# First unit of a gated linear-attention kernel: products of raw neighbours, summed on TensorE and scaled afterwards

## The chip, the cores and the metric

The kernel runs on one core of a Trainium2 chip. That core has five engines, each with its own list of instructions: PE (TensorE, the matrix unit, with PEld for its weight loads), DVE (VectorE), ACT (ScalarE), POOL (GpSimd) and SP (SyncE, which here only issues DMAs). They run side by side and wait for one another by semaphores. The metric is the device time of one execution, in microseconds (us).

## The reference

Two parts follow each other. The first is a recurrence over 768 steps for 4 batches and 8 heads of width 48, with a complex gate per step and channel; the second multiplies its output (3072 rows of 384) by two matrices with a squared ReLU between.

```python
mag = np.sqrt(a_re * a_re + a_im * a_im)
scale = np.minimum(mag, 0.999) / (mag + 1e-06)
a_re_n, a_im_n = (a_re * scale, a_im * scale)
for t in range(S):
    ar, ai = (a_re_n[:, :, t, :, None], a_im_n[:, :, t, :, None])
    new_re = ar * S_re - ai * S_im
    new_im = ar * S_im + ai * S_re
    kv = np.einsum('bhd,bhe->bhde', k[:, :, t], v[:, :, t])
    S_re, S_im = (new_re + kv, new_im)
    y[:, :, t] = np.einsum('bhd,bhde->bhe', q[:, :, t], S_re)
# x: y as 3072 rows of 384
h = x @ w_in
r = np.maximum(h, 0.0)
return (r * r) @ w_out
```

## The kernel before

**Units.** The 3072 rows are cut into six units of 512, `n` = 0 to 5. A unit lies on 128 partitions with four neighbouring steps on each (`c` = 0 to 3) and is treated in two halves of four heads, `z` = 0 and 1. Since a step is a product with a complex gate, a chunk of steps needs the running products of the gates. The kernel forms them in stages:

- `roots(z)`: from the gate `a` (tile `aq`: re and im, 768 elements each per half) the inverse root of its squared length, by squares (L998 on DVE, L993 on ACT), a sum (L1001), logarithm, exponential and square on ACT (L1003, L1005, L1008), and one refining step on DVE (L1011, L1015).
- `normalise(z)`: the scale, from three copies with a factor on ACT (L1021, L1028, L1030) and a minimum times a factor on DVE (L1032); then `a` times the scale (L1035, 1536 wide).
- `inner(z)`: each pair of neighbouring steps multiplied: four real products by L1050 (as two instructions) and their sum and difference by L1054 and L1055; then the product of the two pairs, of which unit 0 forms only the terms on DVE.
- `totals`: in unit 0 PE adds those terms and turns them (`joint`, L1125, with the permuted identity `perm` and its negative); ACT copies the outcome into `e` (L1136, L1139).
- `scan`: 128 totals are multiplied up along the partitions in short steps on DVE (L1211 to L1282). PE turns the outcome back (`back`, L1104, copied by L1303), giving `xn`.
- `moved`: a row of `e` needs the value of the partition before it. Four DMAs on SP's queue (L1195) copy `xn`, shifted by one partition, into `e`; the first partition is set by POOL (L1189). `factors` forms an inverse (L1152 to L1167) whose row moves the same way.
- `inverse` (L1069, L1074), `twist` (L1081) and `apply` (L1351 to L1379) use `e` on `a`, q and k; the last of them write the products to `f`.

Then `pairs` turns those products (in unit 0 on PE, L1494, copied by ACT L1497), multiplies them to scores (L1516), masks them on DVE (L1522), and mixes them with v and the states (L1574, L1578) into `xT`. `dense` follows with w_in (L1634, on `xT`), the squared ReLU on ACT (L1666, L1667), and w_out (L1681 in unit 0, L1743 in the others; these replace one product in eight by sums on DVE, L1758 and L1767).

**Weights.** They arrive as 64-bit floats in 16 pieces, which are fetched on POOL's queue (L826) into buffers that are free then, and converted: the low word on ACT (L839), the sign and top of the mantissa on ACT (L843) or, for the last two pieces, on DVE (L849), the rest on DVE (L845, L852).

**What sets the order.** Every step is recorded by `step` with an assumed duration, the keys it reads and writes, and a rank; `Plan.order` lays all of them out as a list per engine, taking on each engine the step of lowest rank among those it thinks ready. The table at the end of `fast_path` (`plan.shift`) moves single steps and groups of steps by changing their ranks. Where PE would stop for a while, `Plan.emit` writes idle products of `ident` by `ident` (L744) into PE's list; they are real instructions and cannot be skipped. On the chip each engine works off its list in that order.

## Time and profile before

| | us |
|---|---|
| median of three runs (lowest, highest) | 669.27 (668.72, 670.49) |
| profiled execution, its own time | 669.19 |
| span of that execution on the core | 667.5 |
| PE busy, of the span | 648.7 |
| DVE busy | 555.4 |
| ACT busy | 380.1 |
| POOL busy | 155.9 |

The profile counts time from the start of the span. An engine is busy while an instruction of its runs; a matmul of 32-bit floats leaves two records, so counts of PE are twice the instructions of the lists shown below. A row of the timeline gives the start, the duration, the engine, the source line, the operation with output<-inputs, shape and count, and, in brackets, how long the engine had stood idle and what ended that. In the table of stretches the columns are, for each stretch, its length, then busy time and instructions of each engine, TensorE's granted clock (1.00 is full speed), the DMA engines' busy share and GB/s.

### The profile page before, as it was taken

The numbers are of one execution on the slowest core, as the hardware profiler recorded it, in microseconds if no ns is written. First come the engines' busy times: TensorE is split into PE (matmuls) and PEld (weight loads), VectorE is DVE, ScalarE is ACT, GpSimd is POOL, SyncE is SP. The second block draws the span as 40 slices with busy tenths as digits, with TensorE's granted clock in tenths as the row PEclk, the third lists the DMA queues.
The fourth block names the chain that finished last, engine by engine and source line by source line (L and its number), as shares of the span: only waits on it lengthen the run. The fifth ranks groups of instructions, "written<-read, shape, count | busy, mean of one in ns | idle before, by whom it ended". The sixth has DMA issues, their size and how long they took to land.

```text
span 667.5 us, 13612 instructions
## 1 busy us (share of the span) xinstructions
PE 648.7 (97%) x5176; PEld 586.9 (88%) x5176; DVE 555.4 (83%) x1137; ACT 380.1 (57%) x640; POOL 155.9 (23%) x253
## 2 busy tenths in 40 slices
PE   9989999999999899999999999999999999999995
PEld 9988888676768898998989999989989989989995
DVE  6999999999599999888998989997889995248631
ACT  6998589935766336658356558157577253141320
POOL 6321565042110022031143051130040210042100
PEclk9999999999999999999999999999999999999998
DMA  6953649157730136433157253174260243188500
GB/s 201 352 162 103 142 118 319 27 119 168 189 96 1 35 90 157 111 100 91 36 136 177 69 130 69 42 181 126 61 167 25 73 111 83 57 315 275 190 7 25
DMA packets 34948, 82.40 MB, mean 123 GB/s; under 512 B 7956, under 2 KB 13600, under 8 KB 34872
## 3 DMA queue, kind: packets, MB, share of 16 engines
q0 software_dynamic: 17024, 58.60, 31.0%
q1 hardware_dynamic: 15672, 20.63, 12.2%
q10 hardware_dynamic: 2176, 2.20, 1.2%
q8 instruction: 43, 0.70, 0.5%
q14 instruction: 33, 0.27, 0.1%
HBM read 48.76 MB, written 4.72 MB: 80 GB/s over the span
## 4 chain that ended last, share of the span: by engine, by line
PE 66%; DVE 21%; DMA 5%; issue 2%; SPq 1%; ACT 1%; POOL 1%; DVEq 0%; POOLq 0%; ACTq 0%
PE d L1634 28%; PE d L1743 27%; PE sc L1516 3%; PE yp L1574 3%; DVE f L1379 2%; PE yp L1578 2%; DVE f L1050 2%; DMA QT<-aq 2%; PE tr L1546 2%; DMA e<-xn 2%; DVE w L852 1%; DMA aq<-in_q_dram 1%; DVE aq L1035 1%; DVE KC L1231 1%; DVE aq L1463 1%
## 5 line engine op out<-in xcount | busy, mean ns | idle before, releaser
L1634 PE MATMUL d<-xT,w 128*128 128x256 f32 x1104 | 245.9, 380 | 0.4 <-ACT ot L1686 0.4
L1634 PEld LDWEIGHTS d<-xT,w 128*128 128x128 f32 x1104 | 208.0, 190 | 30.5 <-ACT ot L1686 0.8
L1666 ACT ACTIVATE g<-d 128x512 f32<-128x512 f32 x92 | 55.0, 598 | 138.5 <-PE d L1634 122.4
L1743 PE MATMUL d<-w,g 128*128 128x192 f32 x640 | 110.6, 326 | 0.0
L1743 PEld LDWEIGHTS d<-w,g 128*128 128x128 f32 x640 | 104.9, 190 | 0.5
L1743 PE MATMUL d<-T,g 128*128 128x192 f32 x480 | 85.8, 329 | 0.0
L1743 PEld LDWEIGHTS d<-T,g 128*128 128x128 f32 x480 | 78.5, 190 | 1.3 <-DVE ot L1767 0.4
L1758 DVE TENSOR_TENSOR g<-g 128x512 f32<-128x512 f32 x80 | 54.0, 689 | 25.0 <-PE d L1743 19.5
L1704 POOL DMA_DIRECT2D out_dram<-ot x22 | 12.5, 567 | 214.5 <-DVE ot L1767 184.1
L1667 ACT ACTIVATE g<-g 128x512 f32<-128x512 f32 x96 | 60.6, 631 | 3.1
L744 PE MATMUL d<-ident 128*128 128x128 f32 x484 | 56.9, 280 | 1.7 <-POOL ident masks.py:199 1.7
L744 PEld LDWEIGHTS d<-ident 128*128 128x128 f32 x484 | 56.1, 196 | 1.9 <-POOL ident masks.py:199 1.7
L1463 DVE STREAM_TRANSPOSE aq<-f 128x768 f32<-128x768 f32 x40 | 47.9, 1278 | 0.2
L1584 ACT COPY yt<-yp 112x512 f32<-112x512 f32 x24 | 26.6, 1110 | 36.3 <-PE yp L1578 36.1
L1423 POOL DMA_DIRECT2D KC<-f x56 | 35.1, 634 | 47.5 <-DVE f L1379 24.4
L1681 PE MATMUL d<-w,g 128*128 128x384 f32 x128 | 44.0, 491 | 1.7 <-ACT g L1667 1.5
L1379 DVE TENSOR_TENSOR f<-aq 128x768 f32<-128x768 f32 (+1 forms) x56 | 43.9, 838 | 0.5
L1466 ACT COPY QT<-aq 32x512 f32<-32x512 f32 x57 | 35.2, 618 | 8.9 <-DVE aq L1463 6.6
L1522 DVE TENSOR_TENSOR A<-sc,mask 128x512 f32<-128x512 f32 x45 | 29.9, 691 | 12.4 <-PE sc L1516 12.1
L1767 DVE TENSOR_TENSOR ot<-ot,d 128x192 f32<-128x192 f32 x70 | 23.6, 349 | 17.9 <-PE d L1743 17.2
L1681 PEld LDWEIGHTS d<-w,g 128*128 128x128 f32 x128 | 23.7, 190 | 16.5 <-ACT g L1667 1.9
L1516 PE MATMUL sc<-QT 96*64 96x128 f32 (+1 forms) x736 | 37.0, 251 | 0.0
(201 smaller groups left out, 995.6 us busy)
## 6 DMA issues: line engine op xcount, KB each, us to landing
QT<-aq SPq DMA_DIRECT2D x152, 64.0 KB
f<-in_moe_w_in_dram POOLq DMA_DIRECT2D x8, 768.0 KB, 6.7
f<-in_moe_w_out_dram POOLq DMA_DIRECT2D x8, 768.0 KB, 6.7
out_dram<-ot POOLq DMA_DIRECT2D x22, 192.0 KB, 2.2
KC<-f POOLq DMA_DIRECT2D x20, 192.0 KB, 3.9
xT<-yt SPq DMA_DIRECT2D x36, 96.0 KB
aq<-in_q_dram POOLq DMA_DIRECT2D x8, 384.0 KB, 4.5
aq<-in_k_dram POOLq DMA_DIRECT2D x8, 384.0 KB, 5.4
```

The source lines that it names most:

```text
L744: plan = Plan(lambda b: pe.matmul(bank[b][:, 0:C], lhsT=ident, rhs=ident, start=True, stop=True), ["d2", "d1", "d0"], lambda ap: tc.nc.val ...
L1379: lambda j=j, r=r, o=o: dve.tensor_tensor(out=o[:, :, :, r * D:(r + 1) * D], in0=qk[:, j], in1=a[:, r], op=ALU.mult), late[z])
L1423: lambda i=i, queue=queue, lo=lo, hi=hi, a0=a0, a1=a1: queue.dma_start(out=kc[lo:hi, i], in_=nat[a0:a1]),
L1463: lambda nat=nat, dst=dst, j=j: dve.transpose(out=dst[:, j], in_=nat), rank)
L1466: lambda b=b, t=t, T6=T6: act.copy(out=t[32 * b:32 * b + 32, b], in_=T6[32 * b:32 * b + 32, i % 2, b]),
L1516: pe.matmul(sa[r:r + C // 2, j, :, lo:32], lhsT=T[:, j, 1, h, ts(late, C // 2)], rhs=T[:, j, 0, h].rearrange("p (c t) -> p c t", c=W)[:, : ...
L1634: pe.matmul(ps, lhsT=w1[:, f // FP, m, ts(f % FP, C)], rhs=xT[:, n % 2, m, ts(grp, G)], start=(m == 0), stop=(m == NM - 1))
L1666: act.activation(out=o, in_=ps, func=AF.Relu)
L1667: act.activation(out=o, in_=o, func=AF.Square)
L1681: pe.matmul(ps, lhsT=gt[:, f % 2, ts(i, C)], rhs=w2[:, f], start=(f == 0), stop=(f == NF - 1))
L1743: pe.matmul(bank[b][:, 0:DH], lhsT=g4[:, r, j], rhs=w(j), start=first and j == 0, stop=last and j == NT - 1)
L1758: step("DVE", tt(4 * C), gk(x0, h) + gk(x1, h), gk(o, h), lambda: dve.tensor_tensor(out=g4[:, o, sl], in0=g4[:, x0, sl], in1=g4[:, x1, sl] ...
```

## The change

All of it but three edits concerns unit 0.

1. `raw_products`: the neighbours' four real products are formed from the gates as loaded, among the steps of `roots`. PE adds them in PSUM with `ident` and its negative (two matmuls of 384 columns for each of re and im, per half). Once the scale is known, `scaled_products` multiplies the scales of the two neighbours and then the sums from PSUM by that. L1035 is gone in unit 0; the first neighbour of each pair is scaled in `first_factors`, which comes with the steps behind the scan.
2. `normalise`, all units: one copy with a factor and an offset and one minimum times it give the scale, so one of three copies on ACT (L1030) is gone.
3. `roots`, unit 0: the second half's square of the real part goes from DVE to ACT.
4. `moved`, unit 0: `e`'s three rows come from PE, by a matmul with an identity that is shifted by one column (`after`, 384 columns each), and a copy by ACT that adds the first partition's constant (`top`). Four DMAs and three POOL memsets are gone, while POOL sets up `after` and `top` at the start.
5. `convert`: the last two pieces of w_out are converted like the others, with L843 on ACT in place of L849 on DVE.
6. A new table of shifts, so a new order in all units, with the fetches in another order too.

```diff
@@ set-up
+    after = yts[1][:, C:2 * C]
+    top = yts[1][:, 2 * C:2 * C + 3]
+    pool.memset(after[:, 0:1], 0.0)
+    pool.tensor_copy(out=after[:, 1:C], in_=ident[:, 0:C - 1])
+    for j, x_ in enumerate((SCALE, 0.0, SCALE ** -2)):
+        pool.memset(top[:, j:j + 1], 0.0)
+        pool.memset(top[0:1, j:j + 1], x_)
@@ convert
-        mixed = i < 2 * NPIECE - 2
-        if mixed:
-
-            step("ACT", 1.68, keys + [("lo", i)], [("lo", i, 1)], lambda: act.activation(
-                out=part(F16, 1), in_=part(I16, 3), func=AF.Copy, scale=2.0 ** -60), rank)
+        step("ACT", 1.68, keys + [("lo", i)], [("lo", i, 1)], lambda: act.activation(
+            out=part(F16, 1), in_=part(I16, 3), func=AF.Copy, scale=2.0 ** -60), rank)
...
-        if not mixed:
-            step("DVE", tt(PW), keys + wk, wk, lambda: dve.scalar_tensor_tensor(
-                out=bits, in0=hi, scalar=0xC0000000, in1=bits,
-                op0=ALU.bitwise_and, op1=ALU.bitwise_or), rank)
@@ new functions
+        def raw_products(z):
+
+            t = (KC[0][:, 0:2 * Y] if z == 0 else xT[:, 0].rearrange("p m t -> p (m t)"))
+            keys = K if z == 0 else [("xT", 0, m) for m in range(NM)]
+            f = t.rearrange("p (j r g d) -> p j r g d", j=2, r=2, d=D)
+            cut = 2 if z == 0 else 1
+            for u in range(cut):
+                gs = ts(u, W * HH // 2 // cut)
+                x0, x1 = (halves(z)[:, :, gs, y] for y in range(2))
+                for j in range(2):
+                    step("DVE", tt(Y // cut), [("a", z, "r", r, u) for r in range(2)], keys,
+                         lambda x0=x0, x1=x1, j=j, gs=gs: dve.tensor_tensor(
+                             out=f[:, j, :, gs], in0=x0, in1=x1[:, j].unsqueeze(
+                                 1).to_broadcast(list(x0.shape)), op=ALU.mult), first)
+            fx = t.rearrange("p (j r x) -> p j r x", j=2, r=2)
+            for r in range(2):
+                b = ("sc0", "sc1", "tr0", "tr1")[2 * z + r]
+
+                def go(r=r, b=b):
+                    pe.matmul(bank[b][:, 0:DM], lhsT=ident, rhs=fx[:, 0, r], start=True,
+                              stop=False)
+                    pe.matmul(bank[b][:, 0:DM], lhsT=ident if r else minus, rhs=fx[:, 1, 1 - r],
+                              start=False, stop=True)
+                step("PE", 1.3, keys + ([] if r else [("yt", 1)]), [(b,)], go, first)
+
+        def scaled_products(z):
+            sc = col[z][1].rearrange("p (g y d) -> p g y d", y=2, d=D)
+            step("DVE", tt(Y // 2), key(z, 1), key(z, 1), lambda: dve.tensor_tensor(
+                out=sc[:, :, 1], in0=sc[:, :, 0], in1=sc[:, :, 1], op=ALU.mult), first)
+            for r in range(2):
+                b = ("sc0", "sc1", "tr0", "tr1")[2 * z + r]
+                step("DVE", tt(Y // 2) + 0.06, [(b,)] + key(z, 1), [("a", z)],
+                     lambda r=r, b=b: dve.tensor_tensor(
+                         out=halves(z)[:, r, :, 1],
+                         in0=bank[b][:, 0:DM].rearrange("p (g d) -> p g d", d=D),
+                         in1=sc[:, :, 1], op=ALU.mult), first)
+
+        def first_factors(z):
+            sc = col[z][1].rearrange("p (g y d) -> p g y d", y=2, d=D)
+            for r in range(2):
+                step("DVE", tt(Y // 2), [("a", z)] + key(z, 1), [("a", z)], lambda r=r: dve.tensor_tensor(
+                    out=halves(z)[:, r, :, 0], in0=halves(z)[:, r, :, 0], in1=sc[:, :, 0],
+                    op=ALU.mult), late[z])
@@ normalise
             step("ACT", ac(Y), key(z, 3), key(z, 0), lambda: act.activation(
-                out=f0, in_=t, func=AF.Copy, scale=0.999), first)
+                out=f0, in_=t, func=AF.Copy, scale=-0.999e-6, bias=0.999), first)
+            scale = f1 if n == 0 else f0
+            step("DVE", tt(Y), key(z, 0, 3), key(z, 1 if n == 0 else 0),
+                 lambda: dve.scalar_tensor_tensor(
+                     out=scale, in0=t, scalar=1.0 / 0.999, in1=f0,
+                     op0=ALU.min, op1=ALU.mult), first)
...
-            step("ACT", ac(Y), key(z, 2), key(z, 1), lambda: act.activation(
-                out=f1, in_=f2, func=AF.Copy, scale=-1.0, bias=2.0), first)
-            step("DVE", tt(Y), key(z, 0, 1), key(z, 0), lambda: dve.scalar_tensor_tensor(
-                out=f0, in0=f0, scalar=1.0, in1=f1, op0=ALU.min, op1=ALU.mult), first)
+            if n == 0:
+                scaled_products(z)
+                return
@@ moved
+            if n == 0:
+                for j in range(rs.start, rs.stop):
...
+                    step("PE", 0.65, ([("xn", 2, i) for i in range(6)] if j == 2 else
+                                      [("xn", j, z) for z in range(2)]) + [("yt", 1)], [(b,)],
+                         lambda j=j, ps=ps: pe.matmul(ps, lhsT=after, rhs=xn[:, j], start=True,
+                                                      stop=True), rk)
+                    step("ACT", ac(DM), [(b,), ("yt", 1)], [("e", j)],
+                         lambda j=j, ps=ps: act.activation(
+                             out=e.rearrange("p r w g -> p r (w g)")[:, j], in_=ps,
+                             func=AF.Identity, bias=top[:, j:j + 1]), rk)
+                return
@@ table of shifts
-        groups={4: 0.43, 15: 436.02, 16: 7.67, 22: 100.25, 29: -247.66, 33: 0.01, 49: 210.38, 69:
+        groups={11: -98.48, 13: 462.32, 15: 462.32, 16: 443.82, 18: -237.52, 81: -141.6, 84: 547.15,
...
```

The change adds lines, so what was L744 is L751 in the lists of the new kernel, L1035 is L1085, L1050 is L1100, L1125 is L1183, L1211 is L1283, L1351 is L1422, L1104 is L1162; L1032, L1040, L1042, L1048, L1053, L1061 and L1251 there are the new products, sums, scalings and the matmul for `e`.

**PE, from the start to `joint`.** In these rows `d` is the bank of the idle products, `f` and `perm` belong to the first matmuls of `joint`, and `tr_112`, `tr_113` are the banks of the totals. Before, from the first instruction:

```order
L744 MATMUL d_109<-ident 128x128 x121
L1125 MATMUL tr_112<-perm,f_70 64x16x8 x2
L1125 MATMUL tr_112<-yt_89,f_70 64x16x8 x2
L1125 MATMUL tr_112<-perm,f_70 64x16x8
L1125 MATMUL tr_112<-perm,f_71 64x16x8
L1125 MATMUL tr_112<-yt_89,f_70 64x16x8
```

With the change, from the first instruction (the banks `sc` and `tr` hold the sums of the raw products of the first and the second half; `KC` and `xT` hold the products):

```order
L751 MATMUL d_109<-ident 128x128 x34
L1040 MATMUL sc_110<-KC_75,ident 128x384
L1042 MATMUL sc_110<-KC_75,yt_90 128x384
L1040 MATMUL sc_111<-KC_75,ident 128x384
L1042 MATMUL sc_111<-KC_75,ident 128x384
L751 MATMUL d_109<-ident 128x128 x3
L1040 MATMUL tr_112<-xT,ident 128x384
L1042 MATMUL tr_112<-xT,yt_90 128x384
L1040 MATMUL tr_113<-xT,ident 128x384
L1042 MATMUL tr_113<-xT,ident 128x384
L751 MATMUL d_109<-ident 128x128 x28
L1183 MATMUL tr_112<-perm,f_70 64x16x8 x2
```

One run of 121 idle products stood ahead of `joint`. Now 34, 3 and 28 stand there, with eight matmuls of 384 columns between.

**PE, from the totals to the first turn of unit 0's products (L1494 before, L1567 now).** Before:

```order
L744 MATMUL d_109<-ident 128x128 x47
L1104 MATMUL tr_112<-ident,xn 128x128 x3
L744 MATMUL d_109<-ident 128x128 x3
L1104 MATMUL tr_113<-ident,xn 128x128 x3
L744 MATMUL d_109<-ident 128x128 x64
L1494 MATMUL d_107<-ident,f_70 96x128 x4
```

With the change:

```order
L751 MATMUL d_109<-ident 128x128 x46
L1162 MATMUL tr_112<-ident,xn 128x128 x3
L751 MATMUL d_109<-ident 128x128 x3
L1162 MATMUL tr_113<-ident,xn 128x128 x3
L1251 MATMUL tr_112<-xn,yt_90 128x384
L751 MATMUL d_109<-ident 128x128 x4
L1251 MATMUL tr_113<-xn,yt_90 128x384
L751 MATMUL d_109<-ident 128x128 x25
L1251 MATMUL tr_112<-xn,yt_90 128x384
L751 MATMUL d_109<-ident 128x128 x32
L1567 MATMUL d_107<-ident,f_70 96x128 x4
```

`e`'s three rows are matmuls now (L1251), and 110 idle products stand where 114 stood.

**DVE, between the roots and the product of the two pairs, unit 0.** `f` holds roots and scales, `aq` the gates. Before:

```order
L1069 SCALAR_TENSOR_TENSOR f_70<-f_70 128x4x144
L1032 SCALAR_TENSOR_TENSOR f_70<-f_70 128x768
L1035 TENSOR_TENSOR aq_68<-aq_68,f_70 128x1536
L1050 TENSOR_TENSOR f_70<-aq_68 128x768 x2
L1032 SCALAR_TENSOR_TENSOR f_71<-f_71 128x768
L1069 SCALAR_TENSOR_TENSOR f_71<-f_71 128x4x144
L1035 TENSOR_TENSOR aq_69<-aq_69,f_71 128x1536
L845 TENSOR_SCALAR w_66<-KC_76 128x768
L1050 TENSOR_TENSOR f_71<-aq_69 128x768 x2
L1054 TENSOR_TENSOR aq_68<-f_70 128x8x48
L1055 TENSOR_TENSOR aq_68<-f_70 128x8x48
```

With the change:

```order
L1032 TENSOR_TENSOR KC_75<-aq_68 128x2x192 x2
L1000 TENSOR_TENSOR f_71<-f_71 128x768
L1010 SCALAR_TENSOR_TENSOR f_70<-f_70 128x384
L1014 SCALAR_TENSOR_TENSOR f_70<-f_70 128x384
L1032 TENSOR_TENSOR xT<-aq_69 128x768 x2
L1010 SCALAR_TENSOR_TENSOR f_71<-f_71 128x768
L1014 SCALAR_TENSOR_TENSOR f_71<-f_71 128x768
L1071 SCALAR_TENSOR_TENSOR f_70<-f_70 128x768
L1048 TENSOR_TENSOR f_70<-f_70 128x8x48
L849 TENSOR_SCALAR w_66<-g 128x768
L1053 TENSOR_TENSOR aq_68<-sc_110,f_70 128x8x48
L1053 TENSOR_TENSOR aq_68<-sc_111,f_70 128x8x48
```

The raw products of the second half (`xT`) now stand ahead of the last steps of its root, those of the first half earlier still; where L1035 and the neighbours' products and sums stood, there are the scale (L1071), the product of two scales (L1048) and two products with PSUM (L1053). One conversion (L849, L845 before) stands in both.

More of the change, by code (lines that the diff above doesn't have):

```diff
@@ L768, in dma @@
     def dma(q, reads, writes, fn, rank, size, lat=1.8, group=None, dur=None):
-        name, took = ("POOL", 0.67) if q is pool else ("SP", 0.62) if q is sp else ("ACT", 0.53)
+        name, took = ("POOL", 0.67) if q is pool else ("SP", 0.62) if q is sp else ("ACT", 0.6)
         step(name, dur or took, reads, writes, fn, rank, (lat, size), group)
@@ L1083, in chain @@
         E = [("e", 0), ("e", 1), ("e", 2)]
-        nperm = yts[0][:, 0:C]
-        for fn in (roots, normalise, inner):
+        K = [(k_, 0, q_) for k_ in ("KC", "KC0", "KC1") for q_ in range(2)]
+        nperm, minus = (yts[i][:, 0:C] for i in range(2))
+        if n == 0:
+            for i, by in ((1, ident), (0, perm)):
+                step("ACT", 0.25, [], [("yt", i)], lambda i=i, by=by: act.mul(
+                    out=yts[i][:, 0:C], in_=by, mul=-1.0), rank)
+            for z in range(2):
+                roots(z)
+                raw_products(z)
+        for fn in (roots, normalise, inner)[n == 0:]:
             for z in range(2):
                 fn(z)
-                if n == 0 and z == 0 and fn is normalise:
-                    step("ACT", 0.25, key(0, 1), [("yt", 0)], lambda: act.mul(
-                        out=nperm, in_=perm, mul=-1.0), rank)
         ps_ = parts(n)
```

46 lines of the change are left out of this document (27 added, 19 removed), and 37 rows, old and new, of tables (groups, single).

## The prediction

> **What bounds the kernel now.** I read the busy totals first, then the table of stretches, since an average over the run hides stages with different limits.
>
> ```profile
> PE 648.7 (97%) x5176; PEld 586.9 (88%) x5176; DVE 555.4 (83%) x1137; ACT 380.1 (57%) x640; POOL 155.9 (23%) x253
> core 0: us, PE busy (x) PEld busy (x) DVE busy (x) ACT busy (x) POOL busy (x), PEclk, DMA share, GB/s
> 0.00:16.00 16.00, 14.35 (x114) 14.35 (x115) 9.47 (x15) 10.81 (x20) 10.84 (x30) 1.00 0.64 196
> 16.00:55.30 39.30, 37.60 (x357) 36.95 (x357) 37.50 (x86) 37.82 (x54) 11.09 (x19) 1.00 0.78 253
> 55.30:90.10 34.80, 32.59 (x498) 29.70 (x496) 34.26 (x93) 23.30 (x34) 15.85 (x22) 1.00 0.47 108
> 110.00:230.00 120.00, 114.65 (x750) 88.83 (x749) 108.94 (x235) 79.84 (x141) 20.58 (x34) 1.00 0.41 106
> 230.00:660.00 430.00, 429.66 (x3372) 399.72 (x3370) 345.67 (x686) 209.93 (x365) 84.89 (x131) 1.00 0.41 113
> ```
>
> PE's 97% is misleading until its work is named. The timeline of PE shows that for the first 62 us it mostly multiplies ident by ident (L744), which nobody reads:
>
> ```profile
> 1.65 28.84 PE L744 MATMUL d<-ident 128*128 128x128 f32 x242 [1.65 <-POOL ident masks.py:199]
> 30.42 0.44 PE L1125 MATMUL tr<-perm,f 128*64 128x128 f32 x4
> 47.22 14.46 PE L744 MATMUL d<-ident 128*128 128x128 f32 x128
> 62.68 1.96 PE L1494 MATMUL d<-ident,f 128*96 128x128 f32 x16 [1.00 <-DVE f L1379]
> 90.13 1.99 PE L1634 MATMUL d<-xT,w 128*128 128x256 f32 x8
> ```
>
> The dense work starts at 90.13. From 230 to 660 PE idles 0.34 us of 430, and 5.35 us of 120 between 110 and 230. So the span is the time to 90.13, then PE's list, then a tail; what brings the start of the list forward shortens the run, as long as PE is fed. Before 90 the limit is DVE: 37.50 busy of 39.30, then 34.26 of 34.80. Its milestones, from the timeline of DVE:
>
> ```profile
> 4.22 0.56 DVE L998 TENSOR_TENSOR f<-aq 128x384 f32<-128x384 f32 x1 [2.73 <-DMA aq<-in_a_im_dram]
> 5.55 0.56 DVE L998 TENSOR_TENSOR f<-aq 128x384 f32<-128x384 f32 x1 [0.77 <-DMA aq<-in_a_im_dram]
> 8.39 1.83 DVE L998 TENSOR_TENSOR f<-aq 128x768 f32<-128x768 f32 x2 [1.14 <-DMA aq<-in_a_im_dram]
> 13.96 0.96 DVE L1011 SCALAR_TENSOR_TENSOR f<-f 128x768 f32<-128x768 f32 x1 [0.63 <-ACT f L1008]
> 35.46 0.35 DVE L1211 TENSOR_TENSOR KC<-e 128x192 f32<-128x192 f32 x1
> 46.12 0.66 DVE L1282 TENSOR_TENSOR xn<-KC 128x288 f32<-128x288 f32 x1
> 55.32 1.43 DVE L1351 TENSOR_TENSOR f<-aq,e 128x192 f32<-128x192 f32 x5 [0.49 <-DMA e<-xn]
> 87.12 1.27 DVE L1522 TENSOR_TENSOR A<-sc,mask 128x512 f32<-128x512 f32 x2
> ```
>
> The scan runs from 35.46 to 46.78, the use of e starts at 55.32, the last mask of unit 0 ends at 88.39, and PE needs 1.74 us more to the dense work.
>
> **The change, part by part.** Durations, from the groups with each shape apart (columns: count, busy us and mean ns of one):
>
> ```profile
> L1035 DVE TENSOR_TENSOR aq<-aq,f 128x1536 f32<-128x1536 f32 x12 | 21.1, 1756 | 0.4
> L1054 DVE TENSOR_TENSOR aq<-f 128x384 f32<-128x384 f32 x12 | 6.7, 555 | 0.3
> L998 DVE TENSOR_TENSOR f<-aq 128x768 f32<-128x768 f32 x2 | 1.8, 954 | 1.1 <-DMA aq<-in_a_im_dram 1.1
> L852 DVE CUSTOM_DVE_ANT_0 w<-T,w 128x1536 uint16<-128x1536 uint16 x5 | 4.7, 957 | 0.0
> L845 DVE TENSOR_SCALAR w<-w 128x768 uint32<-128x768 uint32 x5 | 2.7, 551 | 0.0
> L849 DVE SCALAR_TENSOR_TENSOR w<-T,w 128x768 uint32<-128x768 uint32 x2 | 1.9, 966 | 0.1
> L1081 DVE TENSOR_TENSOR aq<-aq,f 128x576 f32<-128x576 f32 x12 | 8.7, 750 | 0.0
> ```
>
> Neighbours on DVE overlap by about 0.085 us (the two of 768 at 8.39 take 1.83, not 1.91), so one counts as 1.67, 0.47, 0.87, 0.87, 0.47, 0.88 and 0.67 us in the order of these rows.
>
> *Ahead of the scan, removed:* two L1035 (3.34), four neighbour sums L1054/L1055 (1.88), one square that goes to ACT (0.87): 6.09. *Added:* two products of scales and four scaled neighbours, all 384 wide (6 x 0.47 = 2.82), and 0.14 because the first half's two raw products are cut in four: 2.96. The raw products themselves are the old L1050, moved ahead. Net -3.1. *Idle time:* the four waits above are 5.27 us. The first (2.73) is for data and stays. With raw products in the list, of the others about 0.2 (ACT's square) and 0.8 (the second half's data at 8.39, DVE through its list at about 7.6) are left, and L1011 no longer waits: -1.5. *Put off:* in the new order one L845 and two L852 fewer stand ahead of the scan (-2.2), and one L1081 more (+0.7). Together -6.1: scan at 29.4.
>
> PE has its own floor there, as its idle products are a fixed list. Their price is 28.84/242 per record, two records each, 0.238 us. The wide matmul's price comes from a row of the dense stage:
>
> ```profile
> 113.56 4.04 PE L1681 MATMUL d<-w,g 128*128 128x384 f32 x12
> ```
>
> Two records each again: 0.66 us for 128x384. The eight sums of raw products cost 5.3 us, the 65 idle products left ahead of the perm matmuls 15.5; with the start at 1.65 and some 2.2 us of waiting for the raw products the floor is 24.6, where DVE's last operand (L1100) is also due. From 30.42 to the scan the old kernel took 5.04; so 29.6, and I take that: **-5.9**. Unseen is how late the raw products come: a microsecond late passes on as one, since the 28 idle products behind them can't be skipped. Bounds -0.3 and +2, taken 0.
>
> The four scaled neighbours read PSUM on DVE; the nearest rows are 128x512 with PSUM and without:
>
> ```profile
> L1522 DVE TENSOR_TENSOR A<-sc,mask 128x512 f32<-128x512 f32 x45 | 29.9, 691 | 12.4 <-PE sc L1516 12.1
> L1758 DVE TENSOR_TENSOR g<-g 128x512 f32<-128x512 f32 x80 | 54.0, 689 | 25.0 <-PE d L1743 19.5
> ```
>
> 691 against 689: no surcharge is taken. [...]
>
> *Scan to the use of e.* Added: four L1061 (1.88, half of the scaling that L1035 did). One L1081 is gone (-0.7), and the 0.49 wait. Conversions: as many as before. Net +0.7: first use at 50.1, **-5.2**. The four DMAs are only worth that 0.49, not the 7.1 us from their issue to 55.32:
>
> ```profile
> 48.20 8.07 SPq L1195 DMA_DIRECT2D e<-xn  x4
> ```
>
> DVE filled that time with conversions and the factors, which remain. e through PE and ACT (0.66 and a copy of 0.5 per row of e) must be there by 50.1: in ACT's list the first two copies stand behind the logarithm, the exponential and one sum of squares, about 3 us after DVE's first factor steps end near 45.7, so at 48.9; the third stands behind one conversion, at 52, and the k products want it at about 53. Bounds: 0, or +1.5 if ACT is late by half a conversion's pair; taken 0.
>
> *To the last mask.* One L852 more stands ahead of it: +0.87, so **-4.3**, and dense at 85.8. ACT now has four conversions (an L839 and an L843, some 2.65 each) between e and the copies of the turned products; from 48.9 it is through at about 60. PE's idle products and DVE's first f hold the first turn until about 58.5, it takes 1.96 (the row at 62.68), so ACT comes when it is just over: 0, at worst +0.5.
>
> *Behind 90.* The last two pieces of w_out lose L849 (-1.9 on DVE) and cost ACT two more of these:
>
> ```profile
> 24.30 1.95 ACT L843 ACTIVATE KC<-KC 128x768 f16<-128x768 int16 x1
> 14.70 0.84 ACT L1030 ACTIVATE f<-f 128x768 f32<-128x768 f32 x1
> 90.00:110.00 20.00, 20.00 (x96) 17.31 (x95) 19.66 (x26) 18.41 (x29) 12.68 (x19) 1.00 0.76 214
> 110.00:130.00 20.00, 19.23 (x79) 13.69 (x78) 18.76 (x63) 19.33 (x34) 1.77 (x5) 1.00 0.44 126
> ```
>
> ACT is 37.7 busy of 40 there; +3.9 and -1.7 (two L1030 of unit 1) is 2.2 more, which its 2.3 of idle time can just hold. Bounds 0 and +2.2; taken +0.3, as most of what waits for ACT there is not PE. In later units the dropped L1030 frees an engine that isn't the limit: 0. DVE has 3.1 us less work by unit 2 (6.1 - 3.0, less L1061's 1.9, plus L849's 1.9) and 1.5 less idle, about what PE gains, so PE's 5.35 us of waits up to 230 stay, but for one idle product dropped (0.24): -0.3; bounds -2 and +2.
>
> Sum: -4.3 + 0.3 - 0.3 = **-4.3 us**. The profiled execution took 669.19 with a span of 667.5 (1.7 around it) and lies 0.08 under the median; so 664.9.
>
> **Rivals.** *B, the lead carries on:* DVE, ahead of the order's needs, removes PE's waits to 230 as well, 2 us of 5.35, and ACT costs nothing: -6.6, 662.6. For it: the chain of waits runs through DVE up to 221. Against: it must gain on PE, and its sum says it only keeps up. *C, ACT takes DVE's place:* the whole 2.2 between 90 and 130, and 0.6 of lateness at e or the raw products: -1.5, 667.7. For it: 19.33 busy of 20. Against: the conversions have no user at once. *D, PE waits in units 4 and 5:* the new order puts the perm matmuls of both units 14 matmuls of 256 columns earlier. These rows show the old place and its last operand:
>
> ```profile
> 398.16 0.35 DVE L1055 TENSOR_TENSOR xn<-f 128x192 f32<-128x192 f32 x1
> 399.38 0.82 PE L1104 MATMUL tr<-perm,xn 128*128 128x128 f32 x6
> 493.44 0.35 DVE L1055 TENSOR_TENSOR xn<-f 128x192 f32<-128x192 f32 x1
> 495.74 0.82 PE L1104 MATMUL tr<-perm,xn 128*128 128x128 f32 x6
> 390.32 9.23 PE L1634 MATMUL d<-xT,w 128*128 128x256 f32 x42
> ```
>
> Two records each, 0.43 us, so 6.0 earlier on top of 4.3. The slack was 0.9 and 2.0. DVE's list ahead of these operands is about 4 and 2.5 us shorter, and 1.5 of idle time is gone, so PE would wait some 3.9 in unit 4, and 4.3 in unit 5 if DVE, which takes g's sources and ot from PE, slips with the first wait. In full: -4.3 + 8.2 = +3.9, 673.1; slower than before from 4.3 us of waits on. Against: between 230 and 660 DVE idles 84 us of 430 (part of it behind the last unit), much of it waiting for PE, and every microsecond of it that goes shortens these waits by one.
>
> **How the numbers follow.** Forecast 0.60, B 0.16, C 0.15, D 0.09. A measurement here can tell 0.3%, 2.0 us: 667.3 and 671.3. The forecast, B and a third of C are faster: 0.81; the rest of C and a little of D are same: 0.11; most of D is slower: 0.08. The bounds below the sum add up to 2.6 (0.3, 2 less the 0.3 taken, and ACT's 0.3, with 0.3 more for B): 662.0 after rounding down. Those above add up to 8.2 (2, 1.5, 0.5, 1.9 and 2.3), and as they are separate accidents I take 0.4 of that, 3.3: 668.2. That holds the forecast, B and C and leaves out D.
>
> **What would show it.** Right: the first L1283 at about 29.6, the first L1422 near 50 with no DMA ahead of it, the first dense matmul at 85 to 87, PE idle under 1 us between 230 and 655. Wrong: a dense start after 88 (raw products or e late; then the wait at L1040 or L1422 names it), ACT as PE's releaser by over 2 us between 85 and 130, or PE waiting over 1 us at L1162 behind DVE's xn in units 4 and 5.

## The result and the profile after

The changed kernel took 659.95 us in the median (658.34 to 660.32), against 669.38 for the kernel before beside it: 0.9847 of its time, 95% interval 0.9825 to 0.987. That is 9.4 us less, where 4.4 less were forecast. In a later comparison on one chip it took 658.39, 0.9829 (0.9815 to 0.9843). The profiled execution has a span of 658.0 against 667.5. One execution of all runs below, of `after_other_order`, took 958.67 us at a granted clock of 0.65; the ratios leave it out.

The busy totals and the table of stretches of the changed kernel, in the stretches shown of before:

```profile
PE 644.6 (98%) x5076; PEld 579.5 (88%) x5076; DVE 549.1 (83%) x1140; ACT 374.0 (57%) x635; POOL 151.6 (23%) x258
16.00:55.30 39.30, 36.69 (x321) 34.11 (x320) 37.44 (x104) 37.47 (x54) 9.64 (x15) 1.00 0.70 225
55.30:90.10 34.80, 32.33 (x482) 29.24 (x482) 34.12 (x82) 24.51 (x37) 13.34 (x23) 1.00 0.58 136
110.00:230.00 120.00, 118.78 (x781) 94.34 (x780) 111.90 (x246) 78.69 (x139) 20.15 (x33) 1.00 0.37 102
```

PE's idle time between 110 and 230 is 1.22 us where it was 5.35. The same steps as before in the timelines of DVE and PE:

```profile
29.29 0.35 DVE L1283 TENSOR_TENSOR KC<-e 128x192 f32<-128x192 f32 x1
49.72 1.16 DVE L1422 TENSOR_TENSOR f<-aq,e 128x192 f32<-128x192 f32 x4
83.24 1.27 DVE L1595 TENSOR_TENSOR A<-sc,mask 128x512 f32<-128x512 f32 x2
86.79 0.60 PE L1707 MATMUL d<-xT,w 128*128 128x256 f32 x2
111.43 0.35 DVE L1283 TENSOR_TENSOR KC<-e 128x192 f32<-128x192 f32 x1
213.03 0.66 DVE L1353 TENSOR_TENSOR xn<-KC 128x288 f32<-128x288 f32 x1
650.02 2.77 PE L1816 MATMUL d<-T,g 128*128 128x192 f32 x16
652.82 0.35 DVE L1840 TENSOR_TENSOR ot<-ot,d 128x192 f32<-128x192 f32 x1 [2.25 <-PE d L1816]
```

and the later ones of before, with PE's longest waits behind the dense start (in brackets: how long it stood idle, and what ended that), and, as the last row, what is left of the one at 220.98 in the changed kernel:

```profile
117.59 0.34 DVE L1211 TENSOR_TENSOR KC<-e 128x192 f32<-128x192 f32 x1
153.37 1.56 PE L1681 MATMUL d<-w,g 128*128 128x384 f32 x4 [1.50 <-ACT g L1667]
190.93 0.39 PE L1574 MATMUL yp<-T 128*48 128x128 f32 x2 [0.88 <-DVE T L1522]
220.98 0.52 PE L1104 MATMUL tr<-ident,xn 128*128 128x128 f32 x3 [1.68 <-DVE xn L1282]
221.59 0.68 DVE L1282 TENSOR_TENSOR xn<-KC 128x288 f32<-128x288 f32 x1
658.20 1.46 PE L1743 MATMUL d<-w,g 128*128 128x192 f32 x8
659.70 0.35 DVE L1767 TENSOR_TENSOR ot<-ot,d 128x192 f32<-128x192 f32 x1 [0.94 <-PE d L1743]
212.42 0.52 PE L1162 MATMUL tr<-ident,xn 128*128 128x128 f32 x3 [0.65 <-DVE xn L1353]
```

Up to the dense start, the first matmul with w_in, all went nearly as forecast: 86.79 for 90.13. The surplus comes behind it. Seen from PE, the dense start is 3.34 us earlier, PE's waits from there to its last matmul are 1.73 us for 5.35 (3.62 less), its work between them is the same (0.09 more), and the end, from DVE's last sum to the end of the span, is 2.62 shorter: together 9.49 of the 9.5.

Seen from DVE, unit 2's scan ends at 213.69 where it ended at 222.27, so 8.58 us earlier. From there PE hardly waits in either kernel (0.47 and 0 us), and needs 439.10 us to its last matmul, 437.39 before (1.71 more). The end takes 4.83 us, 7.45 before (2.62 less). -8.58 + 1.71 - 2.62 = -9.49: the spans differ by 9.5.

DVE's 8.6 us by stretches: to unit 0's last mask, to unit 1's scan, through it, and to the last instructions of unit 2's. Before, then changed, each with its sum:

```profile
0.00:88.39 88.39, 82.89 (x938) 79.52 (x938) 79.52 (x192) 71.61 (x105) 37.24 (x70) 1.00 0.63 185
88.39:117.59 29.20, 29.14 (x151) 24.30 (x152) 28.58 (x44) 26.23 (x43) 14.25 (x21) 1.00 0.85 242
117.59:128.80 11.21, 10.68 (x44) 7.57 (x42) 10.24 (x47) 10.70 (x18) 0.00 (x0) 1.00 0.08 13
128.80:220.90 92.10, 87.36 (x620) 66.72 (x617) 82.80 (x158) 55.50 (x97) 19.32 (x30) 1.00 0.42 106
sum 220.90, PE 210.06 PEld 178.11 DVE 201.15 ACT 164.04 POOL 70.81; mean PE 52.52 PEld 44.53 DVE 50.29 ACT 41.01 POOL 17.70
```

```profile
0.00:84.51 84.51, 78.01 (x839) 71.86 (x840) 76.94 (x195) 67.41 (x105) 34.12 (x75) 1.00 0.66 192
84.51:111.43 26.92, 26.69 (x143) 22.60 (x144) 26.37 (x37) 24.93 (x38) 13.29 (x20) 1.00 0.78 203
111.43:123.80 12.37, 12.37 (x43) 7.99 (x42) 11.47 (x49) 12.21 (x12) 0.00 (x0) 1.00 0.28 108
123.80:212.40 88.60, 87.60 (x626) 68.08 (x625) 81.81 (x161) 59.76 (x114) 19.69 (x30) 1.00 0.43 110
sum 212.40, PE 204.67 PEld 170.53 DVE 196.60 ACT 164.31 POOL 67.10; mean PE 51.17 PEld 42.63 DVE 49.15 ACT 41.08 POOL 16.77
```

The stretches shorten by 3.9, 2.3, -1.2 and 3.5 us. In all, DVE's work up to there falls by 201.15 - 196.60 = 4.55 and its idle time by 19.75 - 15.80 = 3.95, of which 2.5 in the last stretch.

### The profile page after: what moved, and what is told of

The parts are those of the page before. It is cut to its first block, busy times and chain, and to the rows that moved or that the text cites. A ratio compares the mean times of both kernels' runs of the same rounds, so it can differ in the third digit from the quotient of the medians.

```text
span 658.0 us, 13402 instructions
## 1 busy us (share of the span) xinstructions
PE 644.6 (98%) x5076; PEld 579.5 (88%) x5076; DVE 549.1 (83%) x1140; ACT 374.0 (57%) x635; POOL 151.6 (23%) x258
## 4 chain that ended last, share of the span: by engine, by line
PE 60%; DVE 10%; issue 1%; ACT 0%; DVEq 0%
PE d L1707 26%; PE d L1816 25%; PE sc L1589 3%; PE yp L1647 2%; PE yp L1651 2%; PE tr L1619 2%; DVE f L1100 1%; DVE aq L1085 1%; DVE g L1831 1%; DVE KC L1303 1%; DVE T L1806 1%; PE tr L1162 1%; DVE f L1071 0%; DVE A L1595 0%; DVE KC L1349 0%
## 5 line engine op out<-in xcount | busy, mean ns | idle before, releaser
L751 PEld LDWEIGHTS d<-ident 128*128 128x128 f32 x362 | 44.3, 203 | 3.4 <-POOL ident masks.py:199 1.6
L751 PE MATMUL d<-ident 128*128 128x128 f32 x362 | 45.2, 287 | 1.6 <-POOL ident masks.py:199 1.6
L1589 PE MATMUL sc<-QT 96*64 96x64 f32 (+1 forms) x736 | 38.2, 252 | 0.0
L1589 PEld LDWEIGHTS sc<-QT 96*64 96x64 f32 x736 | 35.1, 137 | 0.2 <-ACT QT L1570 0.2
```

What stands on the lines that cost most here:

```text
L751: plan = Plan(lambda b: pe.matmul(bank[b][:, 0:C], lhsT=ident, rhs=ident, start=True, stop=True), ["d2", "d1", "d0"], lambda ap: tc.nc.val ...
L1589: pe.matmul(sa[r:r + C // 2, j, :, lo:32], lhsT=T[:, j, 1, h, ts(late, C // 2)], rhs=T[:, j, 0, h].rearrange("p (c t) -> p c t", c=W)[:, : ...
```

## The experiments

The runs carry the name of the kernel that they start from. The table has what all are read by: the start of the dense work, of unit 1's scan and the end of unit 2's scan on DVE, PE's last matmul, what lies between these two, and the end, from DVE's last sum to the end of the span (us, of the profiled executions). The time is the median, the ratio that to the kernel before in the same comparison.

| run | time | ratio (95%) | dense | scan 1 | scan 2 ends | last matmul ends | between | end |
|---|---|---|---|---|---|---|---|---|
| before | 669.27 | 1 | 90.13 | 117.59 | 222.27 | 659.66 | 437.39 | 7.45 |
| before_last_on_act | 669.79 | 1.0003 (0.9991-1.0014) | 90.41 | 117.86 | 223.60 | 660.99 | 437.39 | 7.61 |
| before_front_short | 668.93 | 0.9993 (0.9984-1.0003) | 90.04 | 117.47 | 221.89 | 659.29 | 437.40 | 7.22 |
| before_convert_on_act | 668.29 | 0.9981 (0.9972-0.9991) | 89.88 | 117.32 | 220.32 | 657.74 | 437.42 | 7.27 |
| before_dve_more | 670.48 | 1.0002 (0.999-1.0014) | 90.65 | 119.30 | 223.88 | 661.33 | 437.45 | 7.08 |
| before_other_order | 676.36 | 1.0114 (1.009-1.0138) | 90.29 | 116.45 | 221.12 | 667.69 | 446.57 | 5.42 |
| after_other_order | 668.84 | 0.9992 (0.9978-1.0007) | 86.16 | 117.56 | 222.59 | 659.99 | 437.40 | 6.72 |
| after_order_to_scan | 672.68 | 1.005 (1.003-1.007) | 86.32 | 110.85 | 225.70 | 663.11 | 437.41 | 6.99 |
| after | 659.95 | 0.9847 (0.9825-0.987) | 86.79 | 111.43 | 213.69 | 652.79 | 439.10 | 4.83 |
| after_again | 658.39 | 0.9829 (0.9815-0.9843) | 86.09 | 110.59 | 211.89 | 650.69 | 438.80 | 5.51 |
| after_last_on_sp | 661.46 | 0.9889 (0.9869-0.9909) | 86.22 | 111.86 | 213.95 | 652.79 | 438.84 | 6.72 |
| after_convert_on_dve | 660.86 | 0.987 (0.9854-0.9887) | 86.13 | 111.16 | 215.60 | 654.12 | 438.52 | 5.79 |
| after_dve_more | 661.57 | 0.9891 (0.9871-0.9912) | 86.13 | 111.24 | 214.15 | 652.65 | 438.50 | 5.16 |
| after_dve_plus4 | 663.38 | 0.9906 (0.9887-0.9924) | 86.35 | 112.08 | 217.55 | 656.06 | 438.51 | 5.35 |
| after_e_by_dma | 659.08 | 0.9839 (0.982-0.9859) | 87.16 | 112.09 | 213.05 | 651.59 | 438.54 | 5.42 |
| after_third_copy | 660.43 | 0.9857 (0.9838-0.9875) | 86.12 | 111.82 | 214.64 | 654.14 | 439.50 | 5.17 |
| after_pe_early | 659.16 | 0.9844 (0.9829-0.9858) | 85.74 | 110.87 | 212.59 | 651.40 | 438.81 | 5.01 |
| after_both | 659.53 | 0.9858 (0.9835-0.9881) | 85.38 | 110.58 | 212.29 | 651.10 | 438.81 | 5.91 |

The column "between" is the finding. With the old order behind unit 2's scan it is 437.39 to 437.45 in seven runs, although that scan ends anywhere between 220.3 and 225.7, and PE has no idle time there. With the new order and the changed steps it is 438.5 to 439.5, with 0.2 to 0.5 of idle time. So once that scan is over the rest is a fixed list of PE's, and a change is worth what it does to the end of unit 2's scan, plus what it does to the end. (before_other_order is the exception, and is explained below.) Two executions of the changed kernel differ by 1.8 us at that point, so a single profile can tell no less than that. And there is little more to gain there: in these two PE waits 1.26 and 0.85 us in all between the dense start and that point.

**Steps and order crossed.** Each kernel with the other's order behind the first dense matmul; the list holds the numbers of the steps in that order.

```diff
+BEHIND = [
...
         order = self.order()
+        order = order[:len(order) - len(BEHIND)] + BEHIND
```

> The kernel before, with all its own steps, in its own order up to the first dense matmul; from there on, the steps of every engine stand in the order of the changed kernel (its own third copies for the scale and its own conversions kept beside the steps they belong to; three idle products behind 90 us left out, 0.7 us). Theory O (the new order alone removed PE's waits between 110 and 230, and the shorter end): dense start at about 90 as before, PE's waits in the 140 us behind it down from 5.35 to about 1.2, last output to end of span 4.8 instead of 7.4; total about 669.3 - 0.7 - 4.1 - 2.6 = 661.9, and 664.5 if the end is not the order's. Theory W (less work on DVE and the earlier start removed the waits): waits stay at 5 or more, total about 668 to 669, or more.

> The changed kernel with all its steps, in its own order up to the first dense matmul (86.8); from there on, the steps stand in the order of the kernel before. Theory O: PE's waits in the 140 us behind the dense start are back at about 5, and the end from the last output is back at 7.4, so 660.0 + 4 + 2.6 = 666.6 (664.0 if the end is not the order's). Theory W: the waits stay near 1.2, total 660 to 661, or 662.6 with the longer end.

Theory O foresaw the second run roughly (666.6 for 668.84) and the first not at all. Theory W's "or more" leaves room for the first, but it missed the second. Neither half is worth anything alone: the edits in the old order have the dense start at 86.16, 4.0 us earlier, and no measurable gain in time (0.9992); the new order around the old steps costs 6.9 us. In the changed kernel with the old order PE and DVE show where the lead goes (timelines; the last row is a table of stretches, PE's granted clock third from the right):

```profile
91.74 1.13 PE L1839 MATMUL sc<-xT,w 128*128 128x256 f32 x4 [2.35 <-DVE w L984]
131.09 1.54 PE L1294 MATMUL tr<-ident,xn 128*128 128x128 f32 x6 [3.10 <-ACT ends_of L1500]
117.56 0.36 DVE L1415 TENSOR_TENSOR KC<-e 128x192 f32<-128x192 f32 x1
93.00:96.40 3.40, 3.40 (x10) 2.69 (x9) 3.37 (x4) 2.28 (x4) 3.40 (x6) 0.50 1.03 240
```

Unit 1's scan (L1415 here) starts at 117.56, as it did before (117.59), though unit 0's last mask is 3.9 us earlier. The old list of DVE has the inverse (L1069, L1074), the twist (L1081) and conversions of unit 1 ahead of that scan. The new list has most of the inverse's products and the twist behind it, so there the scan starts 6.2 us earlier. PE, early at the dense work, stops 2.35 us for a conversion and 3.10 for ACT.

DVE's totals up to the end of unit 2's scan part the two causes. It is busy 202.41 of 222.27 us before, 200.12 of 222.59 here, and 197.78 of 213.69 in the changed kernel. So the edits alone take 2.29 us of its work, and it stands idle 2.61 longer; the new order takes 2.34 more of its work and 6.56 of its idle time. Two things account for nearly all of these 8.9 us. Of the six differences of weights that go to `T` (L1733, now L1806; 0.95 us each) two stand behind that scan, where the old order has all six ahead of it. And DVE waits less for ACT: its waits of over 0.4 us from the dense start to that point, all for ACT, come to 11.66 us in this run and to 4.45 in the changed kernel. The timelines of DVE show both, two rows of before and then four of the changed kernel:

```profile
177.98 0.96 DVE L1011 SCALAR_TENSOR_TENSOR f<-f 128x768 f32<-128x768 f32 x1 [6.01 <-ACT f L1008]
208.05 1.82 DVE L1733 TENSOR_TENSOR T<-w,T 128x768 f32<-128x768 f32 x2
168.39 0.96 DVE L1010 SCALAR_TENSOR_TENSOR f<-f 128x768 f32<-128x768 f32 x1 [2.58 <-ACT f L1007]
179.46 0.96 DVE L1000 TENSOR_TENSOR f<-f 128x768 f32<-128x768 f32 x1 [1.86 <-ACT f L978]
215.59 0.95 DVE L1806 TENSOR_TENSOR T<-w 128x768 f32<-128x768 f32 x1
217.06 0.95 DVE L1806 TENSOR_TENSOR T<-w,T 128x768 f32<-128x768 f32 x1
```

The old steps in the new order have 6.37 us of PE's waits behind unit 2's scan, where no other run of the table has more than 0.5, and 4.94 of them are of this form:

```profile
298.03 7.61 PE L1767 MATMUL d<-xT,w 128*128 128x256 f32 x34 [1.29 <-DVE ot L1900]
494.44 3.40 PE L1767 MATMUL d<-xT,w 128*128 128x256 f32 x14 [1.89 <-DVE ot L1900]
```

There DVE's sums (L1900, L1767 of before) are late in units 3 to 5. The new order seems to let PE come to them sooner, and to need a DVE that is ahead; no run shows that by itself.

**The new order up to unit 1's scan only.** The same edit with another cut, the changed kernel's steps, the old order behind that scan.

> The changed kernel with its own order up to the end of unit 1's scan on DVE (near 123.8); from there on all its steps stand in the order of the kernel before (what that order had done already comes first). Theory S (the order's worth lies in what it puts off until behind unit 1's scan: inverse, twist, a conversion): most of the gain stays; unit 2's scan ends near 214 to 216, total 660 to 663. Rival L (the worth lies in the order behind unit 1's scan): unit 2's scan ends at 219 or later, total 665 to 669.

Rival L has the direction, and the result lies beyond its range. So my reading isn't borne out, that what is put off behind unit 1's scan is the whole worth of the order. That scan starts at 110.85, but unit 2's ends at 225.70, later than anywhere. Part of this is the seam itself, where ACT's list is late for both (timelines of PE and DVE):

```profile
127.58 4.63 PE L1831 MATMUL d<-xT,w 128*128 128x256 f32 x12 [6.80 <-ACT g L1863]
130.02 0.96 DVE L976 CUSTOM_DVE_ANT_0 w<-w 128x1536 uint16<-128x1536 uint16 x1 [3.83 <-ACT w L971]
136.51 0.56 DVE L1334 TENSOR_TENSOR KC<-KC 128x384 f32<-128x384 f32 x1 [4.46 <-ACT KC L1329]
181.43 0.96 DVE L1134 SCALAR_TENSOR_TENSOR f<-f 128x768 f32<-128x768 f32 x1 [6.12 <-ACT f L1131]
```

DVE's two waits there are 8.3 us, and unit 2's scan ends 12.0 later than in the changed kernel. So this run can't say how much of the order's worth lies ahead of the scan and how much behind. The last row stands in every run with the old order in that place (3.47 to 6.85 us; 6.01 before): DVE waits for ACT at unit 2's roots. In the new order the two waits there are 2.58 and 1.86.

**Work on DVE behind the dense start.** Edit 5 undone, and edit 5 alone in the kernel before:

```diff
+        def signs():
+            if not last:
+                act.activation(out=part(F16, 1), in_=part(I16, 3), func=AF.Copy, scale=2.0 ** -60)
...
+            if last:
+                dve.scalar_tensor_tensor(out=bits, in0=hi, scalar=0xC0000000, in1=bits,
+                                         op0=ALU.bitwise_and, op1=ALU.bitwise_or)
```

> The changed kernel, order kept, with edit 5 undone: the last two pieces of w_out get their sign and top of the mantissa on DVE again (two instructions, +1.9 us on DVE between about 115 and 130) and not on ACT (two of 1.94 us fewer). Theory W (behind the dense start DVE's list sets when PE can go on, so its work counts one for one): PE's waits from the dense start to 230 rise from 1.3 to about 3.2, total 661.9. Theory A (ACT is the scarcer one there): no more waits, or fewer, total 659.5 to 660. Theory F (the new order has slack there, and edit 5 is worth nothing): 660.0.

> The kernel before, order kept, with edit 5 alone: two DVE instructions fewer (1.9 us), two ACT instructions more (3.9 us) between 115 and 130. Theory W: PE's waits between 128 and 230 (5.35 in all, of which 1.7 at 221 and 0.9 at 191 behind DVE) fall by up to 1.9, total 667.4 to 668. Theory A: the wait at 128 to 153 behind ACT (2.0 of the 5.35) grows by 1 to 4, total 670 to 673. Theory F: 669.4.

In the changed kernel the 1.9 us come back at two places where PE needs a conversion; PE's waits up to unit 2's scan are 3.11 for 1.26, and that scan ends 1.9 to 3.7 later than in the two profiles of the changed kernel:

```profile
125.20 4.14 PE L1762 MATMUL d<-w,g 128*128 128x384 f32 x12 [0.97 <-DVE w L860]
130.24 2.20 PE L1762 MATMUL d<-w,g 128*128 128x384 f32 x6 [0.90 <-DVE w L860]
```

In the kernel before the same edit brings unit 2's scan forward by 1.95, and the time by 1.2 us (0.9981). So edit 5 is worth about 1 to 2 us in either order: DVE's work counts, as theory W had it. But ACT's price is there too: in the old order PE's wait for ACT near 130 (0.53 before) became 2.40. The new order has no such wait.

A conversion's instruction done more often in four pieces, two times and three times:

```diff
+        def top_bits():
+            for _ in range(2 if i >= 2 * NPIECE - 4 else 1):
```

> The changed kernel, order kept; in the last four pieces of w_out one DVE instruction of a conversion (0.55 us, 0.47 of them on the path) is done twice, so DVE has 1.9 us more to do between about 95 and 130 and ACT has the same. Theory W: total 661.9, waits up by about 1.9. Theory F (slack): 660.0. Against the run without edit 5 it tells what ACT's part is: equal totals mean that ACT's 3.9 us are worth nothing.

> The changed kernel, order kept; one DVE instruction of a conversion done three times in the last four pieces of w_out: 3.8 us more on DVE, nearly all between 95 and 130. Theory D (DVE's arrival at the end of unit 2's scan sets the time): that end moves from 213.7 to about 216 to 217.5, and the last matmul by as much less the 0.5 to 1 us of slack: total 662 to 663.5. Rival (DVE's idle time of 9 us between 124 and 212 takes it): total 660.

> The kernel before, order kept; one DVE instruction of a conversion done twice in the last four pieces of w_out: 1.9 us more on DVE. Theory D: the end of unit 2's scan moves from 222.3 to about 224, total 671.0 to 671.4. Rival (PE's list sets the time and its waits of 5.35 are chance): 669.4 to 670.

With 3.8 us more, unit 2's scan ends 3.9 to 5.7 later and the time is 3.4 to 5.0 us longer than the two medians of the changed kernel: one for one, with no slack in DVE's 7 us of idle time behind unit 1's scan. Theory D's 662 to 663.5 holds. DVE's idle time from the dense start to that point is 7.73 us, for 8.31 and 7.37 in the changed kernel, so it is the added work that moves it. With 1.9 more the time is 1.6 to 3.2 longer, but this profile's scan ends at 214.15, only 0.5 to 2.3 later (the profiled execution, at 659.96, was the shortest of the four). In the kernel before no difference can be measured (1.0002), and 223.88 lies beside the 223.60 of a run with nothing added; so theory D is shown in the changed kernel, and left open there.

**Single edits undone, and PE early.** Edit 4 (e by transfers again):

```diff
-                    step("ACT", ac(DM), [(b,), ("yt", 1)], [("e", j)],
...
+                    for lo, hi in ((0, C - 16), (C - 16, C - 1)):
+                        sp.dma_start(out=to[lo + 1:hi + 1], in_=xn[lo:hi, rs])
```

> The changed kernel, order kept, with edit 4 undone: unit 0's e comes by four transfers and three memsets again; the three matmuls and the three ACT copies for it are left out. In the kernel before, the first two rows were usable 7.1 us after their issue and cost DVE 0.49 us of idle time. Here they would be issued near 43 and the use of e stands at 49.7, and the third row, issued near 50, is wanted at 52.9. Forecast (the transfers are hidden but for about half a microsecond): dense start 0.3 to 0.6 later, total about 660.5. Rival (with DVE's list ahead shortened the latency is exposed): DVE idle 1 to 4 us at the use of e, total 661 to 664.

```profile
43.31 8.29 SPq L1250 DMA_DIRECT2D e<-xn  x4
50.10 1.16 DVE L1424 TENSOR_TENSOR f<-aq,e 128x192 f32<-128x192 f32 x4
```

The use of e comes at 50.10 for 49.72, with no wait of DVE's. The dense start is the latest of the changed kernel's runs (87.16), but the time is no longer (659.08). Edit 4 is worth nothing that can be measured: the transfers were hidden.

A copy more on ACT for the scale of units 1 to 5 (edit 2), and the last six idle products left out:

```diff
+                for _ in range(2 if n else 1):
+                    act.activation(out=f0, in_=t, func=AF.Copy, scale=-0.999e-6, bias=0.999)
```

```diff
+            if n in (339, 381):
+                many = 0
```

> The changed kernel, order kept, with one ACT copy of 0.84 us more for the scale of each half of units 1 to 5 (the same copy done twice, and the scale waits for both). Forecast (ACT isn't the limit in later units): no change, 660.0. Rival (the copy lies on the chain from the roots to the scale, which DVE and then PE wait for, above all between 90 and 130, where ACT was 18.3 busy of 20): up to 1.7 us of new waits, total 660.8 to 661.7.

> The changed kernel without its last six idle products (four near 83, two just ahead of the dense start; 1.4 us of PE): PE starts the dense work up to 0.6 us earlier, DVE does what it did. Theory D: PE only waits longer, at the next place where it waits for DVE; total 660.0, unchanged. My forecast's reading (the dense start, then PE's list): total 659.4, and no longer waits.

Neither makes a difference that can be measured. The second has PE at the dense work at 85.74, the earliest but one, and unit 2's scan ends at 212.59, between the two profiles of the changed kernel. PE's earlier start doesn't pass on, as it stands idle 1.43 us up to there, for 1.26 and 0.85.

**A shorter front in the old order.**

```diff
-                    out=part(t, u), in_=part(f1, u), func=AF.Square,
+                    out=part(t, u), in_=part(f1, u), func=AF.Square if n else AF.Copy,
...
+            for _ in range(many - 16 if many == 121 else many):
```

> The kernel before, order kept, with a shorter front: in unit 0 the refining step of the inverse root (six DVE instructions) is left out, so its accuracy is less, and 16 of the 121 idle products in front are left out. Dense start about 3 to 3.6 us earlier, near 86.8. Theory P (a lead at the dense start passes to the end one for one in any order): total about 666. Theory K (an order holds only the lead it was made for; what stands behind, conversions and unit 1's roots, comes no earlier): the lead is given back in waits between 90 and 230, which rise from 5.4 towards 8, total 668 to 669.

It answers another question. The kernel leaves out the refining step of unit 0's roots and 16 idle products. With these six instructions fewer DVE just waits for ACT's copies of the scale, and unit 0's scan starts at 35.33 as before (35.46):

```profile
15.63 0.76 DVE L1069 SCALAR_TENSOR_TENSOR f<-f 128x576 f32<-128x576 f32 x1 [4.36 <-ACT f L1030]
```

ACT's chain behind the roots was about to become the limit there. The change dodges that by its contents: the raw products need no root, so DVE has work while ACT's chain runs, and edit 2 takes one copy out of the chain.

**Which queue carries the last output.**

```diff
-        queue = (act if (i, half) == (1, 0) else sp) if final else pool
+        queue = (act if (i, half) == (0, 1) else sp) if final else pool
```

> The kernel before, with one edit: of the last four output transfers the very last one is issued by ACT and the one before it by SP; it was the other way round. Theory Q (which queue carries the last output sets the length of the end): from DVE's last sum to the end of the span 4.8 us instead of 7.4, total 666.7. Rival F (the end is set by fetches of instructions behind the last transfer, whichever queue carries it): 7.4 stays, total 669.3.

> The changed kernel, with one edit: the last but one of the final output transfers is issued by ACT and the very last by SP; it was the other way round. Theory Q: from DVE's last sum to the end of the span 7.4 us instead of 4.8, total 662.6. Rival F: 4.8 stays, total 660.0.

Half of theory Q holds. In the changed kernel, with the last output on SP, the end is 6.72 us for 4.83 (and the time 1.5 to 3.1 longer). In the kernel before, with the last on ACT, it stays: 7.61. There SP's last transfer is issued 1.3 us ahead of it, in the changed kernel 2.6 ahead:

```profile
650.60 0.33 SPq L1772 DMA_DIRECT2D out_dram<-ot  x1
653.21 0.38 ACTq L1772 DMA_DIRECT2D out_dram<-ot  x1
```

In the runs of the table, the end takes 4.83 to 5.91 us with the last on ACT and SP's last 2.6 us ahead of it (ten runs), and 6.72 to 7.61 otherwise (eight). The two kernels below, without their tables, have the first arrangement too, with 6.01 and 4.85. The new order put the last blocks of w_out so that it holds. What makes the end longer otherwise isn't shown.

**Neither table.** The kernels without their tables of shifts:

```diff
+    plan.shift(groups={}, single={})
```

> The kernel before without its table of shifts: every step in the order that the plain ranks give. With the next run it shows what edits 1 to 5 are worth where no order was fitted to either kernel. Expected some 15 to 40 us above 669.

> The changed kernel without its table of shifts. Theory K (edits and order have to fit; the edits alone are worth little): within 2 us of the kernel before without its table. Theory W (DVE's work and the shorter front pass on in any order): 3.3 for the front and 1 to 3 for the waits, so 4 to 7 us below it.

714.73 and 685.07 us (1.0669 and 1.0228). The gap of 29.7 us is no measure of the edits: the plain ranks led to different idle products (groups by shape: count, busy us and mean ns),

```profile
L744 PE MATMUL d<-ident 128*128 128x128 f32 x682 | 81.0, 281 | 1.6 <-POOL ident masks.py:199 1.6
```

```profile
L751 PE MATMUL d<-ident 128*128 128x128 f32 x460 | 57.2, 285 | 1.6 <-POOL ident masks.py:199 1.6
```

whose busy time alone differs by 23.8 us; how much of that passes on isn't shown. Neither theory named such a gap (within 2 us, or 4 to 7). The pair says that both kernels owe more to a fitted order than to any single step.

**Back and once more.** The changed kernel again, and it with edit 4 undone and without the six idle products.

> The changed kernel once more, beside the next run. Theory D: the end of unit 2's scan within 1 us of 213.7, last matmul 438.5 to 439.5 behind it, end from DVE's last sum 4.8 to 5.8; total 659.5 to 660.5.

> The changed kernel, order kept, with edit 4 undone (e by four transfers) and without the last six idle products. If the two differences of 0.8 and 0.9 us seen in single comparisons are real and add up: 658.3. If they are scatter between executions: within 0.5 us of the run before it.

658.39 and 659.53. The first is 1.1 below the range named for it, with unit 2's scan 1.8 earlier than in the first profile. The second is 1.1 longer, more than the 0.5 that was named for scatter, but not shorter, and the intervals overlap. So the differences of 0.8 and 0.9 don't add up to a gain, and no run points to a version below the changed kernel.

## Why the prediction was wrong

**The front: right but for its last step.** Unit 0's scan starts at 29.29 (forecast 29.6; -6.2 for -5.9), the use of e at 49.72 (50.1). No instruction of the new front waits long: the raw products are in time, and DVE comes to L1053 without a wait. The last mask ends at 84.51 (forecast 84.1). Between the use of e and that mask one L852 more stands, as I had counted (four for three; three L845 or L849 in both), but the stretch is 1.72 us longer and not 0.87: 0.31 of that are short waits, and the other 0.54 is neighbours that overlap less. That is outside the bounds of this step (at worst +0.5). PE needs 2.28 us more to the dense start, not 1.74, behind two idle products that I hadn't put there. So -3.3 for -4.3; the scan's lead of 0.3 covers part of it.

All the signs named for being right came, the last one up to PE's last matmul, and none of those for being wrong. They watched the front and the time behind 230, and the terms that failed lie between 90 and 230 and at the end.

**Operands in PSUM: no surcharge.** The four L1053 took 0.55 us each, L1048 of the same width with none in PSUM 0.56:

```profile
L1048 DVE TENSOR_TENSOR f<-f 128x384 f32<-128x384 f32 x2 | 1.1, 558 | 0.1
L1053 DVE TENSOR_TENSOR aq<-tr,f 128x384 f32<-128x384 f32 x2 | 1.0, 550 | 0.0
```

**e by PE: right**, at nothing, as the run with the transfers shows.

**The step that failed: "so PE's 5.35 us of waits up to 230 stay".** They fell to 1.45 from the dense start to 230. The step rested on the sum of "3.1 us less work by unit 2" and "1.5 less idle". Measured, DVE has 4.55 less work and 3.95 less idle time at the end of unit 2's scan: 8.5 earlier and not 4.6. The mistake was to price the new order at nothing behind the dense start. I had taken DVE's gain as the sum of the edits, and the order as what it does to them. The two crossed runs show the reverse: the same edits in the old order bring unit 2's scan forward by nothing (222.59 for 222.27): there PE stops for a conversion and for ACT, DVE waits for ACT, and DVE's list has other work ahead of unit 1's and unit 2's scans. Of the 3.1 the edits alone bring 2.29, and DVE gives them back in waits. Against that run the new order puts off two differences of weights (1.9 us) and saves 7.2 us of DVE's waits for ACT. Edit 5 in particular I had put at +0.3 for ACT's load; it is worth 1 to 2 us. How much each move of the order is worth between 124 and 213 stays open.

**What bounds it: misread.** I took the span as "the time to 90.13, then PE's list", since PE was busy 95% and more behind it. The chain of waits ran through DVE up to 221, which I noted under rival B and left there. The column "between" shows that the end of unit 2's scan is the point from which PE's list counts. The last of PE's waits, 1.68 us for DVE at 220.98, ties its list to DVE's.

**The end: a second step, at nothing without a reason.** It is 2.6 us between the two profiles, 1.8 between the means of the two groups of runs. I had taken this time as a constant ("then a tail"); the order changed the distance of the last two transfers.

**Rivals.** B (the lead carries on) had the direction and the mechanism, DVE ahead of the order's needs, at 2 us instead of 4. C's mechanism is real in the old order (PE's wait for ACT near 130 went from 0.53 to 2.40 with edit 5 alone), and the new order avoids it; its sum counts ACT's 0.3 twice and should read -1.8. D didn't come: from 230 to its last matmul PE idles 0.3 us (422.51 busy of the 425 to 655, of which 2.21 lie behind the last one), none of it at the perm matmuls of units 4 and 5. Its kind of wait is what the old steps in the new order show (0.5 to 1.9 us each behind DVE, units 3 to 5).

## What to carry to other kernels

Where PE looks saturated but still stops a few times for another engine, look for the last of these stops: what lies behind it was a constant here as long as the order stayed, and a change is worth what it does to that point. A hand-fitted order is a part of the kernel's steps and not an addition to them: here the edits without it brought nothing that can be measured, it without the edits cost 6.9 us, and both together brought 9.4. When an order moves, look at the last few transfers too.
